# Batch 1's attention moved beside group 0's mixer, with loads reordered, v spread in 32-row tiles, and filler matmuls

## The chip, the cores and the metric

The kernel runs on one core of a Trainium2 chip. The metric is the device time of one execution in microseconds, lower is better. A core has five engines with a queue each: TensorE (PE, with its weight loads shown as PEld), VectorE (DVE), ScalarE (ACT), GpSimd (POOL) and SyncE (SP). Each engine works through its queue in order, and engines wait for each other by semaphores. POOL issues the loads that change float32 to bf16; SP issues the other DMAs.

## The reference

Selective attention for 8 batches, 8 heads, 576 positions and head size 64, followed by a mixer on the heads put together (8 x 576 x 512):

```python
cum = np.cumsum(np.maximum(s, 0.0), axis=-1)
bias = -(cum[:, :, :, None] - cum[:, :, None, :])
scores = np.where(causal, -1e9, q @ k.T / np.sqrt(D) + np.minimum(bias, 0.0))
x = softmax(scores) @ v                    # heads side by side: (B, S, 512)
u = x + ((x.transpose(0, 2, 1) @ U) @ V).transpose(0, 2, 1)   # rank 32 over positions
out = u + np.maximum(u @ w_ch1, 0.0) @ w_ch2                   # 512 -> 2048 -> 512
```

`causal` marks the keys behind a query's position.

## The kernel before

Attention goes by pairs of heads: pair `n` is two heads of batch `n // 4`, 32 pairs in all. A pair has three parts, written as generators that hand back control (`yield`) between pieces:

- `transposes(n)`: 16 PE transposes turn q and k (loaded as 72 partitions x 8 rows) into the pair's slot, one of five; the results go from PSUM to the slot by four copies of 64x576, on ACT or DVE as `copies` says. Four more rows of the slot hold the bias: for batch 0 SP copies them from `rows`, later from `rows_hbm`.
- `scores(n)`: for each head one step of 1024 columns, then one step for both heads (`mid`) and a small one (`tail`). ACT makes exp of each into `pT`; a causal mask follows, on POOL for pairs 1 to 3, on DVE elsewhere. Scores use two PSUM buffers (`pscore`); everything else on PE shares four (`pwork`).
- `values(n)`: 30 matmuls with the head's v, whose extra column of ones gives the sum; DVE divides.

When a batch is through, `seqmix(b)` makes the mix over positions (rank 32) and writes u, transposed, into groups of 512 positions (`uT`). Batch 0 has its own form, `mix_first`, one quarter of the 512 channels at a time. `chanmix(g)` is the channel mixer of a group: 16 hidden steps (4 matmuls of 512 columns each, then a relu on ACT), then four output tiles of 16 matmuls in steps of four. Group 0 adds u by four identity matmuls, later groups by DVE.

`chanmix` runs as filler between the pieces of attention. `run(gen)` calls `step_fill` after each piece, and the pace says how many of 8 calls do a step of the oldest chanmix in `fill`. Before, the pace is 3 of 8 in batch 1, 7 of 8 later, and all at the end. Batch 0 is written out by hand (`step`, `drain`), with `spin_some` for filler matmuls on constant data.

v of batch 0 comes by rows of 4 positions per partition (`v_raw`, and `v_raw_end` for the last 64), and `v_tile(j)` spreads it to 128-position tiles with a selecting matrix `sel`: four matmuls of 512 columns, 128 rows deep (16 for the last). Other batches load v straight into `v_slots` in pieces of one head's row. U, V, w1 in halves, w2 whole, then q and k of batch 1 follow v of batch 0 in POOL's queue; v of batch 1 is issued when batch 0's mix is through, and then q, k and v of batch 2.

The order of PE and POOL is the order in which the program is written, for the whole kernel. DVE, ACT and SP are held to it only up to the call of `in_program_order` behind batch 0; a scheduler orders the rest. POOL's loads use eight semaphores in turn, so a load's issue waits for the landing of the eighth load before it.

Of the kernel before, what the change touches and what calls it, by code (L numbers as in the profile page):

```python
# [39 lines left out]
def kernel(  # L40
# [29 lines left out]
    FT = 2  # L70
# [23 lines left out]
    v_raw_end = v_early[:16, 2048:4096].rearrange("p (h t d) -> p h t d", h=H, t=4)  # L94
# [18 lines left out]
    def ones(ap):  # L113
# [24 lines left out]
    nc.gpsimd.dma_start(  # L138
        out=v_raw.rearrange("p h t d -> p h (t d)"),
        in_=v[0, :, 0:512, :].rearrange("h (p t) d -> p h (t d)", t=4),  # L140
    )
    nc.gpsimd.dma_start(
        out=v_raw_end.rearrange("p h t d -> p h (t d)"),
        in_=v[0, :, 512:576, :].rearrange("h (p t) d -> p h (t d)", t=4),
    )

# [13 lines left out]
    nc.vector.memset(keep, 3.0e38)  # L160
    causal(keep, 1, 128)

# [41 lines left out]
    U_sb = consts.tile([128, 5, 128], BF16)  # L204
    V_sb = consts.tile([128, 4, S], BF16)
# [24 lines left out]
    nc.vector.memset(U_sb, 0.0)  # L230
    nc.vector.memset(V_sb[:, 0, :], 0.0)
# [6 lines left out]
    for half in range(2):  # L238
        nc.gpsimd.dma_start(
            out=w1_sb[:, :, ds(half * 1024, 1024)], in_=w1_in[:, :, ds(half * 1024, 1024)]  # L240
        )
    nc.gpsimd.dma_start(out=w2_sb, in_=moe_w_ch2.rearrange("(kt kp) n -> kp kt n", kp=128))
    alloc_qk(1)
    load_qk(1, 0, H)
# [10 lines left out]
    def copies(n, hh, par):  # L255
        b = n // PB
        on_act = n == 0 or (n == 1 and par == 0) or (b == 1 and par == 1)
        return nc.scalar.copy if on_act else nc.vector.tensor_copy

    def transposes(n):  # L260
        b, hp = divmod(n, PB)
        slot = slots[n % NSLOT]
        if b > 0:
# [3 lines left out]
            )  # L267
        for hh in range(2):
            h = 2 * hp + hh
            tp = pwork().bitcast(BF16)[:, : 2 * 4 * TP].rearrange(  # L270
                "p (c t m) -> p c t m", c=2, t=4
            )
            for c, src in enumerate((q_t[b], k_t[b])):
                for t2 in range(4):
                    nc.tensor.transpose(  # L275
                        tp[:, c, t2, :], src[:, h, ds(t2 * 128, 128)], identity[:TP, :TP]
                    )
# [184 lines left out]
    def v_tile(j, copy):  # L462
        src, rows_in = (v_raw, 128) if j < 4 else (v_raw_end, 16)
        pv = pwork()
        for t in range(4):
            nc.tensor.matmul(
                pv.rearrange("p (h d) -> p h d", h=H),
                lhsT=sel[:rows_in, ds((3 + 128 * j if j < 4 else 3) - t, 128)],
                rhs=src[:, :, t, :],
                start=(t == 0),  # L470
                stop=(t == 3),
            )
        copy(v_slots[0][:, j, :, 0:D], pv.rearrange("p (h d) -> p h d", h=H))
# [66 lines left out]

    def chanmix(g, hT=None, done=0):
# [7 lines left out]
        for nf in range(done, NF):  # L549
# [3 lines left out]
            yield  # L553
        for i in range(4):
            f2 = pwork()
            for nf in range(NF):
                nc.tensor.matmul(  # L557
                    f2,
                    lhsT=hT[:, nf, ds(i * 128, 128)],
                    rhs=w2_sb[:, nf, :],  # L560
                    start=(nf == 0),
                    stop=(g > 0 and nf == NF - 1),
                    skip_group_check=True,
                )
                if nf % 4 == 3 and nf < NF - 1:
                    yield
# [25 lines left out]
    pace = [0, 8]  # L592

    def step_fill():
        pace[0] += 1
        if pace[0] % 8 >= pace[1]:
            return
        while fill:
# [17 lines left out]
    def pT_of(n):  # L616
        return pT_early[n - 2] if 2 <= n < PB else pTs[n % 2]

    first_v = v_slots[0]
    nc.vector.memset(first_v[:, 0:4, :, D : D + 1], 1.0)  # L620
# [139 lines left out]
```

## Time and profile before

| what | before |
|---|---|
| median of 6 runs, us | 396.9 (393.95 to 397.84) |
| the profiled execution, us | 396.95 |
| its span, first to last instruction, us | 395.2 |
| mean granted TensorE clock | 0.991 |
| PE busy, us | 374.4 |
| PE weight loads busy, us | 214.1 |
| DVE busy, us | 222.9 |
| ACT busy, us | 194.5 |
| POOL busy, us | 62.4 |

Busy time is the time in which an engine has an instruction under way. Matmuls overlap in PE's pipeline, so a busy PE needn't be at its peak. Times in the text count from the span's start. A stage table gives busy time between two moments; the timeline gives instructions in order, several alike put together, with the idle time before them and what ended it in brackets.

### The profile page before, as it was taken

To read this page: it belongs to the slowest core of one execution; us is meant where nothing else is said; L and a number is where in the kernel's file an instruction comes from. 1 tells how busy PE (TensorE), PEld (TensorE's weight loads), DVE (VectorE), ACT (ScalarE), POOL (GpSimd) and SP (SyncE) were. 2 spreads that over 40 slices of the span, in tenths; PEclk is the share of its full clock that TensorE was granted. 3 is DMA by queue.
4 is the path that set the end of the run, shared out by engine and by line. 5 is a ranking of instruction groups with operands and counts; after the bars stand their busy time and mean duration, and the time that the engine had idled before them with its cause. 6 is when DMAs were issued, how large, how long until landed. Compare 5 with 4: busy or idle time off the path is not lost.

```text
span 395.2 us, 8325 instructions
## 1 busy us (share of the span) xinstructions
PE 374.4 (95%) x3474; PEld 214.1 (54%) x3532; DVE 222.9 (56%) x480; ACT 194.5 (49%) x290; POOL 62.4 (16%) x89
## 2 busy tenths in 40 slices
PE   8899688989999899999999999999999999999995
PEld 3575255755555455555555555455655554444442
DVE  7882045887677766766676667676678352002011
ACT  5865458526733376427632773367434820630610
POOL 8754243200500050005000500000000000000000
PEclk9999969999999999999999999999999999999999
DMA  7999999984995399229932997141224015301002
GB/s 113 184 224 196 153 115 117 177 57 82 125 119 93 83 137 98 75 78 146 112 55 81 136 127 73 57 96 21 46 71 98 17 35 133 81 27 75 6 27 80
DMA packets 89122, 37.78 MB, mean 96 GB/s; under 512 B 70462, under 2 KB 82910, under 8 KB 89086
## 3 DMA queue, kind: packets, MB, share of 16 engines
q0 software_dynamic: 50416, 18.44, 58.9%
q1 hardware_dynamic: 38670, 18.82, 24.6%
q8 instruction: 27, 0.44, 0.5%
q14 instruction: 9, 0.07, 0.1%
HBM read 37.51 MB, written 9.95 MB: 120 GB/s over the span
## 4 chain that ended last, share of the span: by engine, by line
PE 80%; DMA 10%; DVE 3%; ACT 2%; issue 2%; POOL 2%; DVEq 0%; POOLq 0%
PE pwork L557 31%; PE pwork L533 28%; PE pscore L290 9%; DMA k_sd<-in_k_dram 8%; PE pwork L355 6%; PE pwork L275 3%; DMA hT<-in_v_dram 2%; PE pwork L427 1%; ACT pT L315 1%; DVE o_sb L569 1%; ACT slot L280 1%; POOL q_sd L108 1%; POOL k_sd L108 1%; PE pwork L384 1%; ACT pT L322 0%
## 5 line engine op out<-in xcount | busy, mean ns | idle before, releaser
L552 ACT ACTIVATE hT<-pwork 128x512 bf16<-128x512 f32 x140 | 84.9, 607 | 113.7 <-PE pwork L533 113.7
L557 PE MATMUL pwork<-w_sb,hT 128*128 128x512 bf16 x550 | 138.2, 383 | 2.4 <-ACT slot L280 0.9
L533 PE MATMUL pwork<-uT,w_sb 128*128 128x512 bf16 x532 | 134.5, 379 | 1.6
L280 DVE COPY slot<-pwork 64x576 bf16<-64x576 bf16 x114 | 90.7, 799 | 22.0 <-PE pwork L275 19.0
L315 ACT ACTIVATE pT<-pscore 128x1024 bf16<-128x1024 f32 x60 | 61.1, 1026 | 48.1 <-PE pscore L290 47.9
L557 PEld LDWEIGHTS <-hT 128*128 128x128 bf16 x576 | 51.6, 98 | 52.5 <-issue 3.1
L533 PEld LDWEIGHTS <-w_sb 128*128 128x128 bf16 x576 | 50.4, 98 | 48.3 <-DVE uT L409 0.3
L290 PEld LDWEIGHTS <-slot 68*128 68x128 bf16 x576 | 44.2, 98 | 29.6 <-issue 2.9
L290 PE MATMUL pscore<-slot 68*128 68x128 bf16 (+4 forms) x512 | 57.6, 248 | 1.9 <-DMA slot<-hT 0.9
L302 DVE TENSOR_TENSOR pT<-pT,keep 128x512 bf16<-128x512 bf16 (+1 forms) x87 | 30.3, 354 | 51.2 <-ACT pT L315 30.2
L569 DVE TENSOR_TENSOR o_sb<-pwork,u_sd 128x512 f32<-128x512 f32 x32 | 22.1, 691 | 63.1 <-PE pwork L557 45.5
L355 PEld LDWEIGHTS <-pT 128*128 128x128 bf16 x900 | 33.6, 97 | 10.6 <-DVE uT L409 0.7
L355 PE MATMUL pwork<-v_slot,pT 128*128 128x65 bf16 x900 | 35.8, 193 | 0.9 <-DVE o_sb L569 0.5
L322 ACT ACTIVATE pT<-pscore 128x1024 bf16<-128x1024 f32 x30 | 31.2, 1039 | 3.3 <-PE pscore L290 2.7
L365 DVE TENSOR_TENSOR x_sb<-pwork,rec 128x320 bf16<-128x320 f32 x64 | 31.2, 489 | 1.9
L108 POOL DMA_DIRECT2D q_sd<-in_q_dram x11 | 8.7, 793 | 148.1 <-PE pwork L275 137.1
L218 POOL DMA_DIRECT2D v_slot<-in_v_dram x28 | 25.0, 910 | 5.6 <-DMA v_slot<-in_v_dram 2.9
L409 DVE TENSOR_TENSOR uT<-pwork,xT 128x256 bf16<-128x256 f32 (+6 forms) x54 | 19.6, 416 | 6.7 <-PE pwork L427 6.7
L275 PE MATMUL pwork<-identity,k_sd 72*128 72x72 bf16 x256 | 18.8, 199 | 4.0 <-DMA k_sd<-in_k_dram 4.0
L275 PEld LDWEIGHTS <-q_sd 72*128 72x128 bf16 x256 | 15.7, 99 | 12.4 <-issue 1.1
L275 PE MATMUL pwork<-identity,q_sd 72*128 72x72 bf16 x256 | 19.1, 198 | 0.3 <-DVE x_sb L365 0.3
L364 DVE RECIPROCAL rec<-pwork 128x5 f32<-128x5 f32 x64 | 12.1, 190 | 12.2 <-PE pwork L355 11.3
(93 smaller groups left out, 176.1 us busy)
## 6 DMA issues: line engine op xcount, KB each, us to landing
out_dram<-o_sb SPq DMA_DIRECT2D x36, 256.0 KB
q_sd<-in_q_dram POOLq DMA_DIRECT2D x7, 576.0 KB, 9.1
k_sd<-in_k_dram POOLq DMA_DIRECT2D x7, 576.0 KB, 13.8
v_slot<-in_v_dram POOLq DMA_DIRECT2D x28, 128.0 KB, 15.6
w_sb<-in_moe_w_ch_dram POOLq DMA_DIRECT2D x2, 1024.0 KB, 14.5
w_sb<-in_moe_w_ch_dram POOLq DMA_DIRECT2D x1, 2048.0 KB, 28.2
q_sd<-in_q_dram POOLq DMA_DIRECT2D x4, 144.0 KB, 4.8
k_sd<-in_k_dram POOLq DMA_DIRECT2D x4, 144.0 KB, 5.3
```

The source lines that it names most:

```text
L275: nc.tensor.transpose(tp[:, c, t2, :], src[:, h, ds(t2 * 128, 128)], identity[:TP, :TP])
L280: copies(n, hh, par)(dst[:, :, :, :, par], tp[par * D : par * D + D].rearrange("p c t m -> p c m t"),)
L290: nc.tensor.matmul(dst, lhsT=slot[0:KA, hh, ds(S + j * 128, 128)], rhs=slot[0:KA, hh, lo:hi], start=True, stop=True,)
L302: nc.vector.tensor_tensor(dst, dst, keep[:, :, 0:w].to_broadcast([128, n_tiles, w]), op=ALU.min,)
L315: nc.scalar.activation(pT[:, hh, 0:1024], near, EXP, scale=scale)
L322: nc.scalar.activation(pT[:, :, 1024:1536], mid.rearrange("p (a b) -> p a b", a=2), EXP, scale=scale)
L355: nc.tensor.matmul(po[:, i, :], lhsT=pT[:, hh, ds(place(j, i), 128)], rhs=vt[:, j, h, :], start=(j == 0), stop=(j == i), skip_group_check= ...
L365: nc.vector.tensor_tensor(x_sb[:, hp, :, ds(hh * D, D)], po[:, :, 0:D], rec.to_broadcast([128, 5, D]), op=ALU.mult,)
L533: nc.tensor.matmul(f1, lhsT=w1_sb[:, kt, ds(nf * 128, 128)], rhs=u[:, kt, :], start=(kt == 0), stop=(kt == 3),)
L552: nc.scalar.activation(hT[:, nf, :], f1, RELU)
L557: nc.tensor.matmul(f2, lhsT=hT[:, nf, ds(i * 128, 128)], rhs=w2_sb[:, nf, :], start=(nf == 0), stop=(g > 0 and nf == NF - 1), skip_group_c ...
L569: nc.vector.tensor_tensor(o_sb.rearrange("p (a b) -> p a b", a=4), f2.rearrange("p (a b) -> p a b", a=4), u_sd[:, :, i, :], op=ALU.add,)
```

## The change

- Batch 1: the order is written out. Three hidden steps of group 0 instead of twelve run alone, then transposes, scores, v tiles and values of batch 1 with the rest of `chanmix(0)` at 8 of 16 calls; pair 8's scores alternate with `seqmix(1)`. Its output tiles 0 and 1 are begun with the first half of w2.
- The pace is a sum (`pace[0] += pace[1]`, a step at 16): 13 of 16 from batch 2 on.
- Loads: w1's first half, q and k of heads 0 to 3 of batch 1, w1's second half, w2 in two halves, q and k of heads 4 to 7. v of batch 1 comes as `v_raw`, and is spread by PE as batch 0's is.
- `v_tiles` replaces `v_tile`: tile j uses only its 32 rows of `v_raw`, and tiles go two at a time with their matmuls alternating; the end tile is 32 rows deep with two matmuls. Copies are on DVE or ACT as the call says.
- Batch 0: q's transposes of a pair stand ahead of k's, slot copies are shared by head between ACT and DVE, memsets move from DVE to POOL, the mix's steps are shifted by one, and 45 filler matmuls stand where 25 stood.
- The clearing and filling of V_sb's other rows stand behind `in_program_order`, and behind the load of `v_raw` for batch 1.

```diff
-    nc.vector.memset(keep, 3.0e38)
+    U_sb = consts.tile([128, 5, 128], BF16)
+    V_sb = consts.tile([128, 4, S], BF16)
+    nc.gpsimd.memset(keep, 3.0e38)
     causal(keep, 1, 128)
+    nc.gpsimd.memset(U_sb, 0.0)
+    nc.gpsimd.memset(V_sb[:, 0, :], 0.0)
...
+    load_v_raw(0)
...
-    for half in range(2):
+    def load_w1(half):
...
-    nc.gpsimd.dma_start(out=w2_sb, in_=moe_w_ch2.rearrange("(kt kp) n -> kp kt n", kp=128))
+    def load_w2(half):
...
+    load_w1(0)
     alloc_qk(1)
-    load_qk(1, 0, H)
+    load_qk(1, 0, 4)
+    load_w1(1)
+    load_w2(0)
+    load_w2(1)
+    load_qk(1, 4, 4)
...
-        on_act = n == 0 or (n == 1 and par == 0) or (b == 1 and par == 1)
+        on_act = hh == 0 and (n < 2 or b == 1)
...
+        if b == 0:
+            for hh in range(2):
+                turn(hh, 0)
+            yield
         for hh in range(2):
...
+            if b > 0:
+                turn(hh, 0)
+            turn(hh, 1)
...
-    def v_tile(j, copy):
-        src, rows_in = (v_raw, 128) if j < 4 else (v_raw_end, 16)
-        pv = pwork()
+    def v_tiles(b, js, copies):
+        vt = v_slots[b % 3]
+        pvs = [pwork() for _ in js]
         for t in range(4):
...
+            for j, pv in zip(js, pvs):
+                if j < 4:
+                    pick, src = sel[ds(32 * j, 32), ds(3 + 128 * j - t, 128)], v_raw[ds(32 * j, 32)]
+                elif t < 2:
+                    pick, src = sel[:32, 3 - 2 * t : 3 - 2 * t + 256 : 2], v_raw_end
+                else:
+                    continue
+                nc.tensor.matmul(
+                    pv.rearrange("p (h d) -> p h d", h=H),
+                    lhsT=pick,
+                    rhs=src[:, :, t, :],
...
+        for j, pv, copy in zip(js, pvs, copies):
+            n_rows = 128 if j < 4 else 64
+            copy(vt[:n_rows, j, :, 0:D], pv[:n_rows].rearrange("p (h d) -> p h d", h=H))
...
+        ahead = {}
+        if g == 0:
+            for i in range(2):
+                ahead[i] = pwork()
+                for _ in outputs(ahead[i], hT, i, range(8)):
+                    yield
+                yield
...
     def step_fill():
-        pace[0] += 1
-        if pace[0] % 8 >= pace[1]:
+        pace[0] += pace[1]
+        if pace[0] < 16:
             return
+        pace[0] -= 16
...
     def pT_of(n):
-        return pT_early[n - 2] if 2 <= n < PB else pTs[n % 2]
+        if n < PB + 3:
+            return pTs[n % 2] if n % PB < 2 else pT_early[n % PB - 2]
+        return pTs[(n + 1) % 2]
...
-    for pT in (*pTs, pT_early[0]):
-        nc.vector.memset(pT[:, :, 1600:], 1.0)
+    init_v(nc.gpsimd, first_v)
+    for pT in (*pTs, pT_early[0]):
+        nc.gpsimd.memset(pT[:, :, 1600:], 1.0)
...
     spin_some(9)
-    for n, spins in ((0, (2, 4)), (1, (3, 3))):
-        for hh, _ in enumerate(transposes(n)):
-            spin_some(spins[hh])
-    drain(transposes(2))
-    step(S0, S0)
+    step(T0)
+    spin_some(2)
+    step(T0, T0)
+    spin_some(8)
+    step(T1)
+    spin_some(4)
+    step(T1, T1)
+    spin_some(6)
+    step(S0)
+    spin_some(1, pwork)
+    step(S0, T2)
+    spin_some(1, pwork)
+    step(T2, T2)
     spin_some(1, pwork)
     step(S0, S0)
+    spin_some(2, pwork)
+    step(T3)
     spin_some(1, pwork)
-    step(S1)
-    drain(transposes(3))
+    step(T3, T3, S1)
+    spin_some(2, pwork)
     step(S1)
     spin_some(2, pwork)
     step(S1, S1)
-    v_tile(0, dve)
+    spin_some(2, pwork)
     step(S2)
-    v_tile(1, dve)
+    spin_some(2, pwork)
+    v_tiles(0, (0, 1), (dve, dve))
     step(S2)
-    v_tile(2, dve)
+    spin_some(1, pwork)
+    v_tiles(0, (2, 3), (act, act))
     step(S2, S2)
-    v_tile(3, dve)
...
+    spin_some(1, pwork)
+    v_tiles(0, (4,), (dve,))
+    nc.gpsimd.memset(pT_early[1][:, :, 1600:], 1.0)
+    step(S3, S3)
...
+    step(M2)
     hidden_first(0)
-    step(M2, M3)
+    step(M3)
     hidden_first(1)
...
+    in_program_order(tc, traced, [E.DVE, E.Activation, E.SP])
+    load_v_raw(1)
+    init_v(nc.gpsimd, v_slots[1])
     nc.gpsimd.memset(V_sb[:, 1:4, :], 0.0)
...
-    in_program_order(tc, traced, [E.DVE, E.Activation, E.SP])
-    load_v(1)
...
+    fill_with(3)
     pace[1] = 8
-    fill_with(12)
-    pace[1] = 3
     run(transposes(PB))
-    for n in range(PB, NP + 2):
+    run(transposes(PB + 1))
+    run(scores(PB, pT_of(PB)))
+    run(transposes(PB + 2))
+    run(scores(PB + 1, pT_of(PB + 1)))
+    run(transposes(PB + 3))
+    run(scores(PB + 2, pT_of(PB + 2)))
+    for js in ((0, 1), (2, 3), (4,)):
+        v_tiles(1, js, (act, dve))
+        step_fill()
+    run(values(PB, pT_of(PB)))
+    run(transposes(2 * PB))
+    run(scores(PB + 3, pT_of(PB + 3)))
+    run(values(PB + 1, pT_of(PB + 1)))
+    run(values(PB + 2, pT_of(PB + 2)))
+    run(values(PB + 3, pT_of(PB + 3)))
+    run(transposes(2 * PB + 1))
+    first, mix = scores(2 * PB, pT_of(2 * PB)), seqmix(1)
+    for _ in range(4):
+        step(first)
+        step_fill()
+        step(mix)
+        step_fill()
+    run(mix)
+    fill.append(chanmix(1))
+    pace[1] = 13
+    for n in range(2 * PB, NP + 2):
...
-                pace[1] = 7
-    pace[1] = 8
+    pace[1] = 16
```

## The prediction

> **What bounds the kernel now.** I read the page's slices first, then a table of stages, then the timeline inside the stages that aren't full, because a share over the whole span (95% PE) hides where the time could come from.
>
> ```profile
> span 395.2 us, 8325 instructions
> PE   8899688989999899999999999999999999999995
> PEclk9999969999999999999999999999999999999999
> ```
>
> PE is at nine tenths from slice 10 on. What the change can win lies in the first 90 us, and in what little is loose behind them. The stage table (columns: PE, PEld, DVE, ACT, POOL busy us with counts, granted clock, DMA share, GB/s):
>
> ```profile
> 12.10:27.20 15.10, 14.14 (x177) 9.40 (x179) 13.11 (x25) 12.52 (x16) 8.68 (x14) 1.00 1.19 210
> 35.30:45.50 10.20, 10.15 (x54) 4.66 (x52) 1.33 (x4) 7.80 (x13) 0.83 (x1) 1.00 1.78 183
> 45.50:49.70 4.20, 0.55 (x8) 0.31 (x7) 0.00 (x0) 0.72 (x2) 1.61 (x4) 1.00 3.47 122
> 49.70:58.60 8.90, 7.74 (x61) 4.34 (x63) 3.68 (x6) 4.99 (x6) 3.90 (x5) 0.62 2.56 113
> 58.60:72.40 13.80, 12.45 (x177) 8.55 (x176) 8.34 (x21) 10.67 (x14) 6.21 (x8) 1.00 2.12 130
> 88.70:391.30 302.60, 296.29 (x2628) 166.01 (x2676) 168.66 (x354) 142.25 (x220) 23.54 (x28) 1.00 0.62 80
> ```
>
> At 35.3 batch 0 is done and twelve hidden steps run alone; from 45.5 PE waits for k of batch 1, which lands at 49.6; behind the wait the clock is 0.62. At 88.7 both kernels will have done the same set of work: group 0's mixer, values of pairs 4 to 7, seqmix(1), scores up to pair 8, transposes up to pair 9. So I predict when that point comes, and then what the last 302.6 us lose or gain.
>
> Per matmul in dense stretches: 0.216 us for 512 columns (four of L533 in 0.86 us), 30 of L355 in 0.91, 12 of L290 in 0.89, 8 transposes in 0.26. From 35.3 to 88.7 the work by these prices is: 28 fill steps of 0.86 and four identity groups of 0.22, 25.1; five pairs of scores at 1.38, 6.9; six of transposes at 0.52, 3.1; four of values, 3.6; seqmix(1) 2.8: 41.5 of 53.4 us. So 11.9 us is loose: 4.2 waiting, about 3 the slow clock, the rest like this:
>
> ```profile
> 58.62 1.02 ACT L322 ACTIVATE pT<-pscore 128x1024 bf16<-128x1024 f32 x1 [0.62 <-PE pscore L290]
> 59.54 0.27 ACT L328 ACTIVATE pT<-pwork 128x128 bf16<-128x128 f32 x1
> 59.83 0.80 ACT L280 COPY slot<-pwork 64x576 bf16<-64x576 bf16 x1
> 60.66 1.02 ACT L315 ACTIVATE pT<-pscore 128x1024 bf16<-128x1024 f32 x1
> 61.71 0.80 ACT L280 COPY slot<-pwork 64x576 bf16<-64x576 bf16 x1
> 62.53 1.02 ACT L315 ACTIVATE pT<-pscore 128x1024 bf16<-128x1024 f32 x1
> 63.45 1.02 ACT L322 ACTIVATE pT<-pscore 128x1024 bf16<-128x1024 f32 x1
> ```
>
> ACT stands end to end: a pair of batch 1 costs it 3.35 us of exp and 1.6 of copies, and no hidden step's relu (0.607, L552) is even among them yet. Batch 0's end hangs on ACT too:
>
> ```profile
> 15.88 1.99 ACT L315 ACTIVATE pT<-pscore 128x1024 bf16<-128x1024 f32 x2
> 26.85 0.27 ACT L328 ACTIVATE hT<-pwork 128x128 bf16<-128x128 f32 x1
> 27.18 1.07 PE L355 MATMUL pwork<-v_slot,hT 128*128 128x65 bf16 x30
> 22.96 1.03 PE L466 MATMUL pwork<-hT,sel 16*128 16x512 bf16 x4
> ```
>
> Pair 2's values take the buffer that pair 3's last exp (end 27.12) frees, and start at 27.18. From there to 35.3 PE is full.
>
> **The change part by part.**
>
> *Batch 0.* Pair 0's first exp starts at 12.76 because the first row DMA lands at 12.1; SP still issues those at 8.2, so that stays. Slot copies of pairs 0 and 1 are split between ACT and DVE and end near 11.6, under that wait: no gain. Memsets go from DVE to POOL: nothing, DVE idled there.
> What is new is the PE queue between exps. Pair 2's transposes now stand before pair 0's third score step: it starts 14.45, exp 15.1 instead of 14.65, last exp ends 16.4. Pair 3's transposes stand before pair 1's first scores (they stood behind), and in the built program's waits the second needs the buffer of that last exp (16.4), and the filler between its q and k halves needs the buffer of pair 2's first copies on DVE: those come behind two masks, 15.2 plus two of 0.83, 16.9. So filler 17.1, k half 17.3, scores 17.8, exp 18.0: 2.1 late against 15.88. The 20 added fillers are 4.3 us of PE, mostly under such waits; this one holds the queue, and behind it stand pair 1's scores, for which ACT waits.
> Two v copies go to ACT (0.6 each) into this chain, and v tiles 0 and 1 (then 2 and 3) become one block before the next score. Before, ACT also lost 1.0 to 23.9 waiting for rows_hbm; that is swallowed. Chain with the v blocks at 1.73 each: pair 1 ends 21.3, pair 2's second exp 23.5 to 24.5, v copies to 26.5, pair 2 ends 27.8, pair 3 31.1. Pair 2's values start 31.15, +4.0. M2's second half now follows its first directly and waits 0.4 for DVE's copy. Batch 0 ends 39.7: **+4.4**. POOL, moved past more: w1's second half, w2's two and q/k's second half are issued behind v_raw's landing (about 17.5), five of 0.8, then ten memsets under 2 us: masks from 24; it needs pair 3's last exp only at 31.1, so 7 us of slack. Behind it POOL issues v_raw(1) and clears V_sb (1.54), which DVE copies 0.93 before M3's copy: ready 37.0, M3 asks for it at 36.6: counted in the rounding.
>
> *The v blocks* are the disputed price. Row: L466 above, 16 rows deep, four in 1.03 with 0.38 the last one's own: 0.217 each, no cheaper than with 128 rows. The Trainium skill, TensorE: Matmul & The Clock Gate (Part 3), says tiles on different row groups run concurrently, 3.07 times for four; TensorEngine Tiling (Key Properties) says a change of tiling mode drains TensorE. Ends: 0.86 and 1.73 per pair. At 0.86 pair 3's exps end 30.0 and batch 0 is +3.3, and batch 1's tiles cost 1.7 less. The trace has no two row groups side by side; I take 1.73, the row, and keep 0.86 for the range: 2.8 us in all.
>
> *Batch 1, part A.* Call batch 0's end P. Three hidden steps, then transposes and scores of pairs 4 to 6 with nine more. The 4.2 us wait and the slow clock go: k of heads 0 to 3 is queued ahead of three quarters of the weights, heads 4 to 7 in the place where all of k was, without v's small pieces: before P+10, when pair 6 asks. What is late next is ACT. Its queue from P+3.4 (relus of the hidden steps before): 8 copies 6.4, 9 relus 5.5, three pairs of exp 10.1, gaps 0.3: 22.3, to P+25.7. PE's own work there is 14.8 us, but two score buffers tie it: pair 6's third step waits for an exp at P+22.8. The clock page (Part 1) drops the clock after an idle window of 3.4 us; the row behind a 4.2 us wait shows 0.62, and 58.6 to 72.4 with ACT leading shows 1.00. Gaps here are near 1 us, so I take 1.00.
>
> *Part B* is PE's from P+23.3: 16 output steps 13.8, identities 0.9, v 3.9, values 3.6, transposes 1.0, two pairs of scores 2.8, seqmix(1) 2.8: 28.9, and 1.2 in waits for v's buffers and copies. End P+53.4, or P+51.7 with cheap tiles. Before: 35.3 + 53.4. So the whole stage gives **0.0**: 12 us of looseness went, 6 came back as ACT's queue, 5 as v, the rest as waits.
>
> *Behind it.* Pace 14/16 becomes 13/16. Per batch 39 calls gave 34.1 steps where a chanmix has 32, so seqmix(2) runs bare:
>
> ```profile
> 130.93 0.23 PE L397 MATMUL pwork<-identity,uxT 128*128 128x128 bf16 x1 [0.64 <-DVE uxT L393]
> 131.54 1.04 PE L427 MATMUL pwork<-V_sb,ux 128*128 128x512 bf16 x4 [0.38 <-DVE ux L399]
> ```
>
> Now 31.7: two output steps stand in these gaps, and one in seqmix(5)'s. PE's waits behind 90 us sum to 3.4; I take **-1.8**, ends -0.5 and -2.5. The tail is dense either way.
>
> Sum: 4.4 + 0.0 - 1.8 = +2.6. The profiled run took 396.95 (span 395.2, 1.75 around it), the median of six is 396.9. So 399.5.
>
> **The rivals.**
> *Cheap tiles, no change.* The v pairs overlap: +3.3 - 1.7 - 1.8 = -0.2, 396.7. For: the page. Against: the row, and three blocks that each change mode twice.
> *Faster.* Batch 0's exp chain isn't held: pair 2's copies on DVE finish before pair 3's filler asks, so pair 1's exp starts by 16.3, 0.4 late. With cheap tiles batch 0 then ends 1.7 sooner: +1.6 - 1.7 - 1.8 = -1.9, and fewer waits in part B than my 1.2 make -2.5: 394.5. It decides at 17 us: an exp of pair 1 before that, and it is faster. Against: the two masks and 0.83 a copy are rows of this trace.
> *Slower by more.* 14.8 of 20.7 us busy is too little, and the clock falls in part A: PE's work doubles to 29.6 there, 9 beyond ACT's: up to 405. For: the 0.62 row. Against: 1.00 from 58.6 on.
> *It doesn't do what it says.* k of heads 4 to 7 still comes at 49.6, as k does now; pair 6 asks at 50, so even that costs nothing.
>
> **How the numbers follow.** The sum as it stands, 0.37; cheap tiles, 0.27; the chain unheld, 0.28; the clock, 0.08. A measurement of this kernel can tell about 0.5%, 2 us. Faster by more 0.28, within 0.27, slower 0.45. The sum's own range is 396.7 to 402 (tiles 2.8 down, 2.5 up for stalls in A and B that I set at 1.2 and the fill). The range of 8 in 10 reaches to the unheld chain with a larger gain behind, 393.0, and into the clock's case, 403.5.
>
> **What would show it.** Right: pair 1's first exp near 18, pair 3's last near 30 to 31, batch 0's end near 39, ACT without gaps for 22 us behind it, no wait for k, granted clock 1.00 from 40 on, the common point at 91 to 93, seqmix(2) with no gap over 0.3. Wrong: pair 1's exp before 17, ACT with gaps in part A, eight v matmuls in under 1 us, or a slice of PEclk under 9.

## The result, and the profile after

The changed kernel takes 392.6 us (median of 29 runs, 391.81 to 396.45) against 396.45 (66 runs, 393.76 to 398.4). The medians differ by 3.9 us; the ratio of the means is 0.9916, 95% interval 0.99 to 0.9932: about 3.3 us faster. The ratios, here and below, leave out executions over 1.5% above the fastest of their kernel, which only e8 (four of twelve) and e15 (two of six) have. The prediction had 399.5, with 393.0 as its lower end. The profiled execution took 393.28 us, span 391.6, so the spans differ by 3.6.

The page first: PE's hole in the fifth slice is gone, and with it the lower clock in the sixth.

```profile
span 391.6 us, 8401 instructions
PE   8799879999999999999999999999999999999995
PEclk9999999999999999999999999999999999999999
```

The stage table (columns: PE, PEld, DVE, ACT, POOL busy us with counts, granted clock, DMA share, GB/s) is cut at the changed kernel's own marks: the first scores, the values of pair 2, the end of batch 0, the end of part A, and the common point, which is here the start of pair 10's transposes.

```profile
12.86:29.80 16.94, 15.73 (x202) 10.24 (x204) 11.25 (x21) 13.29 (x18) 12.60 (x25) 1.00 1.21 211
29.80:38.40 8.60, 8.36 (x120) 5.80 (x120) 5.08 (x18) 2.76 (x6) 6.42 (x12) 1.00 1.21 209
38.40:61.40 23.00, 19.51 (x181) 10.93 (x181) 9.69 (x17) 22.57 (x34) 6.79 (x8) 1.00 2.02 169
61.40:88.35 26.95, 25.82 (x320) 16.31 (x324) 20.51 (x47) 8.24 (x11) 3.32 (x4) 1.00 1.52 93
88.35:391.00 302.65, 294.82 (x2638) 165.63 (x2684) 168.81 (x352) 141.75 (x220) 23.50 (x28) 1.00 0.63 81
```

Both kernels have done the same work when pair 10's transposes start. These are the rows of that point, first before and then after, and before's first scores:

```profile
88.24 0.29 PE L275 MATMUL pwork<-identity,q_sd 72*128 72x72 bf16 x4
88.35 0.29 PE L292 MATMUL pwork<-identity,q_sd 72*128 72x72 bf16 x4
12.11 0.62 PE L290 MATMUL pscore<-slot 68*128 68x128 bf16 x6
```

The 88.7 of the prediction is the first hidden step of group 1 (88.74 in that trace), and half of pair 10's transposes stand ahead of it: it is half a us late as a common point. So batch 0 ends at 38.4 (before: 35.3, +3.1). From there to the common point it is 50.0 us (before 52.9, -3.0). Behind it 391.6 - 88.35 = 303.25 us are left (before 395.2 - 88.24 = 306.96, -3.7). The sum is the 3.6 of the spans. Three readings lie behind these three numbers.

Batch 0, from the timeline (start, duration, engine, line, what it does; in brackets the idle time before it and its releaser):

```profile
12.86 0.60 PE L319 MATMUL pscore<-slot 68*128 68x128 bf16 x6 [1.56 <-DMA slot<-hT]
16.80 0.29 PE L292 MATMUL pwork<-identity,q_sd 72*128 72x72 bf16 x4 [0.44 <-ACT pT L357]
17.58 0.38 PE L191 MATMUL pwork<-busy 128*128 128x512 bf16 x1 [0.49 <-DVE slot L309]
18.70 1.94 ACT L344 ACTIVATE pT<-pscore 128x1024 bf16<-128x1024 f32 x2 [1.95 <-PE pscore L319]
21.71 1.08 PE L502 MATMUL pwork<-hT,sel 32*128 32x512 bf16 x8
22.73 0.62 PE L319 MATMUL pscore<-slot 68*128 68x128 bf16 x6
29.86 1.07 PE L384 MATMUL pwork<-v_slot,hT 128*128 128x65 bf16 x30
```

Pair 3's q half waits for the last exp of pair 0, the filler behind it for DVE's copies of pair 2, and pair 1's first exp is late by that: 18.70, with ACT idle for 1.95 us. The eight v matmuls are through in 1.02 us, from 21.71 to the next instruction's 22.73. Pair 2's values start at 29.86. The first row DMA also landed later than before, so the first scores start at 12.86 in place of 12.11; counted from them batch 0 takes 25.5 us in place of 23.2, 2.3 more.

Part A, one period of ACT from the first exp of pair 4 to that of pair 5:

```profile
45.90 1.94 ACT L344 ACTIVATE pT<-pscore 128x1024 bf16<-128x1024 f32 x2
47.71 0.62 ACT L603 ACTIVATE hT<-pwork 128x512 bf16<-128x512 f32 x1
48.19 1.06 ACT L351 ACTIVATE pT<-pscore 128x1024 bf16<-128x1024 f32 x1
49.09 0.32 ACT L357 ACTIVATE pT<-pwork 128x128 bf16<-128x128 f32 x1
49.25 0.65 ACT L603 ACTIVATE hT<-pwork 128x512 bf16<-128x512 f32 x1
49.73 1.65 ACT L309 COPY slot<-pwork 64x576 bf16<-64x576 bf16 x2
51.40 0.60 ACT L603 ACTIVATE hT<-pwork 128x512 bf16<-128x512 f32 x1
51.89 1.93 ACT L344 ACTIVATE pT<-pscore 128x1024 bf16<-128x1024 f32 x2
```

ACT has no gap, as predicted. But the durations of the first seven rows sum to 6.84 us and the period is 5.99: an instruction starts 0.11 to 0.17 before the ACTIVATE ahead of it ends. Behind the two copies there is no such overlap (49.73 + 1.65 = 51.38, next start 51.40).

Behind the common point, all the waits of PE that the table of waits lists (total, times, longest):

```profile
PE pwork L413 <- DVE x_sb L394: 0.4, 1, 0.4
PE pwork L456 <- DVE ux L428: 0.4, 1, 0.4
PE pwork L384 <- DVE uT L438: 0.4, 1, 0.4
PE pwork L479 <- DVE uT L438: 0.3, 1, 0.3
```

That is 1.5 us where 3.4 stood before. At seqmix(2), where before's lines show waits of 0.64 and 0.38, two output steps now stand in the gaps and PE does not wait.

### The profile page after: what moved, and what is told of

Its sections match the earlier page's. It is cut to its first block, busy times and chain, and to the rows that moved or that the text cites. A ratio compares the mean times of both kernels' runs of the same rounds, so it can differ in the third digit from the quotient of the medians.

```text
span 391.6 us, 8401 instructions
## 1 busy us (share of the span) xinstructions
PE 374.2 (96%) x3507; PEld 213.2 (54%) x3568; DVE 224.9 (57%) x472; ACT 193.8 (49%) x293; POOL 64.1 (16%) x99
## 4 chain that ended last, share of the span: by engine, by line
PE 89%; ACT 5%; DVE 2%; issue 1%; DMA 1%; ACTq 0%; DVEq 0%
PE pwork L581 31%; PE pwork L571 29%; PE pscore L319 10%; PE pwork L384 7%; PE pwork L292 3%; PE pwork L456 2%; ACT pT L344 1%; PE pscore L191 1%; PE pwork L502 1%; DMA slot<-hT 1%; ACT hT L603 1%; DVE x_sb L394 1%; PE pscore L571 1%; PE pwork L413 1%; ACT slot L309 1%
## 5 line engine op out<-in xcount | busy, mean ns | idle before, releaser
L571 PE MATMUL pwork<-uT,w_sb 128*128 128x512 bf16 x530 | 136.1, 379 | 2.6 <-ACT pT L357 0.9
L581 PE MATMUL pwork<-w_sb,hT 128*128 128x512 bf16 x548 | 136.0, 379 | 1.4 <-issue 0.2
L309 DVE COPY slot<-pwork 64x576 bf16<-64x576 bf16 x116 | 92.8, 800 | 11.6 <-PE pwork L292 9.8
L344 ACT ACTIVATE pT<-pscore 128x1024 bf16<-128x1024 f32 x58 | 58.6, 1025 | 47.5 <-PE pscore L319 47.1
L319 PE MATMUL pscore<-slot 68*128 68x128 bf16 (+4 forms) x512 | 56.1, 245 | 3.5 <-DMA slot<-hT 1.6
L319 PEld LDWEIGHTS <-slot 68*128 68x128 bf16 x576 | 43.2, 97 | 29.2 <-issue 6.1
L384 PEld LDWEIGHTS <-pT 128*128 128x128 bf16 x870 | 32.8, 98 | 11.3 <-issue 0.8
L384 PE MATMUL pwork<-v_slot,pT 128*128 128x65 bf16 x870 | 35.3, 193 | 0.8 <-DVE uT L438 0.4
L351 ACT ACTIVATE pT<-pscore 128x1024 bf16<-128x1024 f32 x29 | 30.2, 1041 | 2.7 <-PE pscore L319 1.9
L223 POOL DMA_DIRECT2D v_slot<-in_v_dram x24 | 21.3, 902 | 14.1 <-DMA w_sb<-in_moe_w_ch_dram 7.7
L292 PE MATMUL pwork<-identity,q_sd 72*128 72x72 bf16 x256 | 18.3, 197 | 1.0 <-ACT slot L309 0.5
L292 PE MATMUL pwork<-identity,k_sd 72*128 72x72 bf16 x256 | 17.8, 197 | 0.0
```

The lines of the kernel that those rows point to most:

```text
L292: nc.tensor.transpose(tps[hh][:, c, t2, :], src[:, 2 * hp + hh, ds(t2 * 128, 128)], identity[:TP, :TP],)
L309: copies(n, hh, par)(dst[:, :, :, :, par], tp[par * D : par * D + D].rearrange("p c t m -> p c m t"),)
L319: nc.tensor.matmul(dst, lhsT=slot[0:KA, hh, ds(S + j * 128, 128)], rhs=slot[0:KA, hh, lo:hi], start=True, stop=True,)
L344: nc.scalar.activation(pT[:, hh, 0:1024], near, EXP, scale=scale)
L351: nc.scalar.activation(pT[:, :, 1024:1536], mid.rearrange("p (a b) -> p a b", a=2), EXP, scale=scale)
L384: nc.tensor.matmul(po[:, i, :], lhsT=pT[:, hh, ds(place(j, i), 128)], rhs=vt[:, j, h, :], start=(j == 0), stop=(j == i), skip_group_check= ...
```

## The experiments

Ratios are of means, to the kernel before as it ran beside each, with 95% intervals; the changed kernel itself has 0.9916. "P" is the end of batch 0.

| run | median us | ratio |
|---|---|---|
| e1 changed, pace 14/16 | 394.33 | 0.9955 [0.9936, 0.9975] |
| e2 before, pace 13/16 | 392.36 | 0.9893 [0.9851, 0.9936] |
| e3 changed, pair 3's transposes one step later | 392.04 | 0.9888 [0.9857, 0.9919] |
| e4 changed, v blocks tile by tile | 392.42 | 0.9899 [0.9868, 0.9929] |
| e5 changed, old order in batch 0 | 391.47 | 0.9897 [0.9866, 0.9929] |
| e6 changed, without fillers | 396.25 | 1.0001 [0.9979, 1.0023] |
| e7 before, k early | 392.15 | 0.9914 [0.9886, 0.9941] |
| e8 changed, v pair on the same 32 rows | 398.1 | 1.0021 [0.9989, 1.0052] |
| e9 before, k early and pace 13/16 | 387.99 | 0.9799 [0.9762, 0.9836] |
| e10 changed, plain v ahead of V_sb | 398.31 | 1.0049 [1.0027, 1.0071] |
| e11 = e5 with q, k of heads 4-7 ahead of w2 | 390.97 | 0.9868 [0.9834, 0.9902] |
| e12 = e11 with e10's load | 396.46 | 1.0008 [0.9984, 1.0032] |
| e13 changed, plain v behind V_sb | 390.18 | 0.9853 [0.9827, 0.988] |
| e14 changed, batch 1's copies on DVE | 390.11 | 0.9861 [0.9834, 0.9889] |
| e15 = e9 with paired v tiles in batch 0 | 389.84 | 0.9815 [0.9769, 0.9862] |
| e16 = e13, e14 and q, k ahead of w2 | 392.16 | 0.9885 [0.9843, 0.9927] |
| e17 = e16 with the old order in batch 0 | 393.09 | 0.9928 [0.9902, 0.9954] |

### The pace alone, both ways

```diff
 # e1, on the changed kernel
-    pace[1] = 13
+    pace[1] = 14
 # e2, on the kernel before
-                pace[1] = 7
+                pace[:] = [0, 13]
```

In e2 the step is counted in sixteenths from there on; the 3/8 of batch 1 stays.

> The changed kernel with its steady pace of 13/16 put back to 14/16, nothing else. Theory (pace): the 3.25 us gained behind the common point at 88.35 come from the slower pace, which leaves output steps for the waits of seqmix(2) and seqmix(5). Then 1.8 to 3.3 us come back: about 394.4 to 396, ratio to the kernel before 0.995 to 0.999, and seqmix(2) shows PE waits of 0.4 to 0.6 us for DVE's uxT and ux again. Rival (the gain behind is the clock's or comes from another order of the first 88 us): under 0.5 us lost, 392.6 to 393.1, ratio 0.991 to 0.993.

> The kernel before with one part of the change alone: from group 1 on the pace 13/16 in place of 7/8; the 3/8 of batch 1 stays as it was. Theory (pace): it gains what the changed kernel gained behind 88 us, 1.8 to 3.3 us: 393.2 to 394.7, ratio 0.992 to 0.9955; everything before 88.7 stays. Rival: the pace is worth under 0.5 us by itself, ratio 0.999 to 1.0.

e1 loses 1.7 us by the medians and 1.9 behind the common point (393.8 - 88.63 = 305.17, against 303.25). The wait of seqmix(2) is back: here are e1's common point and its step of seqmix(2), and the same step in the changed kernel.

```profile
88.63 0.30 PE L292 MATMUL pwork<-identity,q_sd 72*128 72x72 bf16 x4
130.71 0.23 PE L426 MATMUL pwork<-identity,uxT 128*128 128x128 bf16 x1 [0.56 <-DVE uxT L422]
128.99 0.22 PE L426 MATMUL pwork<-identity,uxT 128*128 128x128 bf16 x1
```

e2's span is 391.3, 3.9 us under before's. This is its common point:

```profile
87.40 0.30 PE L275 MATMUL pwork<-identity,q_sd 72*128 72x72 bf16 x4
```

Behind it 303.90 us follow in place of 306.96: 3.1 us. The other 0.8, ahead of it, is not the edit's, as nothing there was changed; it is how far two executions of the same work differ. The pace is a gain by itself, and by the medians it is worth as much in the kernel before as the whole change. But e2 also sets the counter to 0 there. Counted from the calls, the changed kernel and e1 come to this point with 0 too, the kernel before with 3 of 8. So e1 changes the pace alone, e2 the pace and this phase; the phase alone was not run.

### The order of loads alone, and with the pace

```diff
 # e7, on the kernel before; e9 adds e2's pace
-    for half in range(2): ...w1 half...
-    nc.gpsimd.dma_start(out=w2_sb, ...)
-    alloc_qk(1)
-    load_qk(1, 0, H)
+    load_w1(0)
+    alloc_qk(1)
+    load_qk(1, 0, 4)
+    load_w1(1)
+    nc.gpsimd.dma_start(out=w2_sb, ...)
+    load_qk(1, 4, 4)
```

> The kernel before with the order of loads alone changed: q and k of heads 0 to 3 of batch 1 stand behind the first half of w1, those of heads 4 to 7 behind w2, as in the changed kernel; v of batch 1, the program order of batch 1 and the pace 7/8 stay. Theory (wait and clock): the 4.2 us that PE waits for k at 45.5 go and with them the stretch at clock 0.62 (about 3 us); ACT's queue takes some of it back: the common point comes 3 to 6 us before 88.7, time 391 to 394, ratio 0.984 to 0.993. Rival (the wait is only moved: ACT's end to end work of batch 1 beside a pace of 3/8, or k of heads 4 to 7 at 49.6, holds PE): under 1.5 us, ratio 0.996 to 1.0.

> The kernel before with two parts of the change and no other: the order of loads (k of heads 0 to 3 early) and the pace 13/16 from group 1 on. Batch 0's order, v of batch 1 by plain loads, and batch 1's program order with its pace of 3/8 stay as before. By the profiles the loads took 6.0 us from the first 88 us and nothing behind them, the pace 3.7 behind and nothing ahead. Theory (the parts add, and what else the change does costs what is missing): span 395.2 - 6.0 - 3.7 = 385.5, time about 387.3, up to 390 in runs where a wait slows the clock; ratio 0.976 to 0.984, 4 us or more below the changed kernel. Rival (both parts fill the same looseness, so one eats the other): 390.5 to 392, ratio 0.986 to 0.990.

e7's common point is the first row here, e9's the second:

```profile
82.21 0.30 PE L279 MATMUL pwork<-identity,q_sd 72*128 72x72 bf16 x4
82.79 0.30 PE L279 MATMUL pwork<-identity,q_sd 72*128 72x72 bf16 x4
```

In e7 it comes 6.0 us before 88.24, with nothing behind it changed (389.2 - 82.21 = 307.0). Its runs spread with the clock: 390.8 to 390.9 where the mean granted clock was 1.0, 393.7 to 394.1 where it was 0.99, and all runs of the kernel before lie at 0.982 to 0.995. In e9 the two gains add but for about half a us: span 386.7, 5.5 us sooner at the common point and 303.9 behind it, 3.1 less than before. At 388.0 us e9 beats both kernels: the changed one by 4.6 us. So load order and pace give more than the change has in all, and what else it does costs 4.6.

### What else it does: batch 0's order

```diff
 # e3: one step moved
-    step(T3)
-    spin_some(1, pwork)
-    step(T3, T3, S1)
+    step(S1)
+    step(T3)
+    spin_some(1, pwork)
+    step(T3, T3)
 # e5: the order of the kernel before
-    spin_some(6)
-    step(S0)
...
-    step(T3, T3, S1)
-    spin_some(2, pwork)
-    step(S1)
+    step(T2, T2, T2)
+    spin_some(4)
+    step(S0, S0)
+    spin_some(1, pwork)
+    step(S0, S0)
+    spin_some(1, pwork)
+    step(S1)
+    step(T3, T3, T3)
+    step(S1)
 # e11: e5, and in the loads
+    load_qk(1, 4, 4)
     load_w2(0)
     load_w2(1)
-    load_qk(1, 4, 4)
```

> The changed kernel with pair 3's transposes and the filler between their halves behind the first scores of pair 1, where they stood before; pair 2's transposes and all fillers stay. Theory (held queue): that block holds pair 1's scores on PE for DVE's copies. Without it pair 1's first exp starts at 16.5 to 17.0 in place of 18.70, pair 3's last exp ends 1 to 2 us before 29.80, batch 0 ends 1 to 2 us before 38.39, and as the stage behind it is full, the time falls by the same: 390.6 to 391.6, ratio 0.9865 to 0.989. Rival (the v copies on ACT and the v blocks cost batch 0 its 3.1 us, or the block is only late elsewhere): batch 0's end moves by under 0.5 us, ratio 0.990 to 0.993.

> The changed kernel with the order of the kernel before at the head of batch 0: pair 2's transposes ahead of pair 0's scores, under the wait for the row DMA; pair 3's in one piece behind pair 1's first scores, with no filler between their halves; one filler where there were one or two. The v blocks, and all behind them, stay as changed. Theory (held queue): what delays pair 1 is the filler and the q half of pair 3's transposes, which wait for pair 2's copies. Pair 1's first exp then starts at 15.9 to 16.7 with the second directly behind it, batch 0 ends 1.5 to 2.4 us sooner than the 37.7 to 38.4 of the changed kernel, and the time is 390.3 to 391.2, ratio 0.984 to 0.988. Rival (once pair 1 comes sooner, the v blocks and the two v copies on ACT, or v_raw's landing, hold pair 2): batch 0's end moves by under 0.7 us, time 392 to 392.6.

> The changed kernel with the old order at the head of batch 0 (as in the run with the old turns) and with q and k of heads 4 to 7 of batch 1 queued ahead of w2. In the run with the old turns PE waited 1.92 us for q of heads 4 to 7 at 46.3 to 48.2 and the granted clock behind it was 0.79 and 0.53 in two stretches of 5 us. Theory (the 2 us won in batch 0 ran into that transfer): now the wait is gone, clock 1.00 throughout, and the time is 390 to 390.8, ratio 0.983 to 0.986, in every run. Rival (another wait comes in its place, w2's above all): 391.3 to 393.

e3 was a miss. Its timeline shows ACT:

```profile
16.09 1.03 ACT L344 ACTIVATE pT<-pscore 128x1024 bf16<-128x1024 f32 x1
18.60 1.02 ACT L344 ACTIVATE pT<-pscore 128x1024 bf16<-128x1024 f32 x1 [1.48 <-PE pscore L319]
```

The first exp of pair 1 came sooner, as expected, but the second stood behind the same block, so the hold had only moved: P is 37.59, and 37.67 in e4, where this order isn't touched. Both differ from the changed kernel's 38.39 mostly because the row DMA landed 0.5 to 0.7 us sooner; counted from the first scores batch 0 takes 25.3 us in e3 and 25.5 in the other two. In e5 the copies are early, since pair 2's transposes lie under the wait for that DMA: exps of pair 1 from 15.74 without a gap, P = 36.18, 2.2 us sooner, of which 0.65 is the row DMA's (24.0 us from the first scores, 1.6 less). By the medians 1.1 us of it are left. The timeline, and e5's stages of 5 us:

```profile
48.20 0.42 PE L292 MATMUL pwork<-identity,q_sd 72*128 72x72 bf16 x4 [1.92 <-DMA q_sd<-in_q_dram]
45.00:50.00 5.00, 3.08 (x28) 1.75 (x26) 1.35 (x4) 3.69 (x7) 2.45 (x3) 0.79 1.59 182
50.00:55.00 5.00, 5.00 (x25) 2.68 (x24) 1.91 (x4) 3.54 (x5) 0.87 (x2) 0.53 1.83 179
```

Pair 6's transposes now ask for q of heads 4 to 7 before it lands at 48.2, and the clock falls behind the wait. (In the changed kernel's profile it lands at about 47.0 and is asked for at 48.33.) This profile is of the slowest of e5's six executions, 393.9 us at a mean clock of 0.991; the two at 1.0 took 390.8 and 390.9. With that transfer ahead of w2 (e11) the wait is gone, the clock is 0.996 or more in every run, and 390.97 is 1.6 us under the changed kernel, a little above the 390 to 390.8 expected: PE waits 1.2 us for ux_first there. That is about the 1.6 us that the order takes from batch 0.

### The fillers

```diff
 # e6: between step(S0) and step(S3, S3)
-    spin_some(1, pwork)   (and all others there: 16 matmuls, one less than the expectation counts)
```

> The changed kernel without the 17 filler matmuls between pair 0's first scores and pair 3's (those ahead of pair 0's scores stay). Theory (the fillers hold the queue a little and keep nothing up): pair 1's first exp at 17.3 to 17.7 in place of 18.0 to 18.7, batch 0 ends 0.3 to 1 us sooner, granted clock 1.00 in every slice, time 391.6 to 392.3. Rival (the fillers keep the clock): slices 1 to 4 of the granted clock fall under 9, batch 0 ends 1 us or more later, time 393.5 or more.

The rival held. Pair 1's first exp starts at 16.53, 2.2 us sooner than in the changed kernel, and yet batch 0 ends 2.3 us later (40.73) and 3.7 us are lost. The first row is a stretch of the changed kernel, the second the same stretch of e6, and behind them are e6's stages of 3 us:

```profile
14.00:17.40 3.40, 2.59 (x36) 1.68 (x35) 2.31 (x4) 2.63 (x4) 2.37 (x4) 1.00 1.49 219
14.00:17.40 3.40, 1.72 (x32) 1.34 (x30) 2.92 (x5) 2.32 (x4) 2.46 (x5) 0.97 1.49 231
15.00:18.00 3.00, 1.83 (x27) 1.43 (x27) 2.94 (x4) 1.92 (x4) 2.06 (x3) 0.86 1.45 260
18.00:21.00 3.00, 3.00 (x19) 1.56 (x17) 2.91 (x6) 2.58 (x4) 2.93 (x5) 0.50 1.08 198
21.00:24.00 3.00, 3.00 (x17) 0.98 (x14) 1.78 (x3) 1.02 (x1) 2.94 (x11) 0.50 1.16 212
27.00:30.00 3.00, 3.00 (x41) 2.55 (x39) 0.99 (x3) 1.94 (x2) 1.36 (x4) 0.50 1.15 211
```

The last column but two is the granted clock: 0.50 from 18 to 30. No single wait of PE's ahead of the drop is longer than 1.21 us, but PE was busy for only 1.72 of the 3.4 us from 14.0 to 17.4, against 2.59 in the changed kernel. All twelve runs have a mean clock of 0.974 to 0.982.

### The v blocks

```diff
 # e4: the two loops exchanged
-        for t in range(4):
-            for j, pv in zip(js, pvs):
+        for j, pv in zip(js, pvs):
+            for t in range(4):
 # e8: both tiles of a block from one row group
+                    at = 32 * (j - j % 2)
-                    pick, src = sel[ds(32 * j, 32), ...], v_raw[ds(32 * j, 32)]
+                    pick, src = sel[ds(at, 32), ...], v_raw[ds(at, 32)]
```

> The changed kernel with the two loops of a v block exchanged: the four matmuls of the first tile, then the four of the second, so that neighbours are on the same 32 rows. Same instructions, same count. Theory (two row groups run beside each other): the block of 8, which took 0.98 to 1.02 us from its start to the next instruction's, takes 1.6 to 1.75; two blocks in batch 0, where pair 2's scores stand behind them and ACT waits, and two in batch 1 where PE is the bound: 1.5 to 3 us more, 394 to 395.5, ratio 0.995 to 0.999. Rival (a matmul of 32 rows is cheap by itself, and the order does not matter): the block stays at 1.0, time 392.6, ratio 0.991 to 0.993.

> The changed kernel with both tiles of a v block taken from the same 32 rows, so v's tiles 1 and 3 get other rows of v; count, shapes and order of the instructions stay, only the second tile's row group is the first's. Theory (two row groups run beside each other, whatever the order): on one group the 8 matmuls run one after the other, 0.216 us apart: the block takes 1.73 us in place of 0.98 to 1.02, pair 2's second scores come 0.75 us later, batch 0 ends 0.7 to 1.5 us later and batch 1's blocks cost 1.5 more: time 394 to 395.3. Rival (a 32-row matmul is cheap by itself): the block stays at 1.0, time 392.2 to 392.8.

The timelines of e4 (first two rows) and e8:

```profile
20.99 1.08 PE L502 MATMUL pwork<-hT,sel 32*128 32x512 bf16 x8
22.00 0.61 PE L319 MATMUL pscore<-slot 68*128 68x128 bf16 x6
21.69 1.90 PE L503 MATMUL pwork<-hT,sel 32*128 32x512 bf16 x8
23.52 0.62 PE L319 MATMUL pscore<-slot 68*128 68x128 bf16 x6
```

On one row group the block takes 1.83 us, on two 1.01, whatever the order in the program: e4's 1.6 to 1.75 was a miss, and e8's row is from a stretch with a clock of 1.00 (21 to 24 us). Two row groups do run beside each other, and a 32-row matmul is not cheap by itself. e8's two runs with a mean clock of 0.998 or more took 394.65 and 395.94, in and just above the 394 to 395.3 expected; the others had 0.978 to 0.996.

### v of batch 1, and ACT's copies

```diff
 # e10; e13 puts load_v(1) behind the V_sb copies instead
-    load_v_raw(1)
-    init_v(nc.gpsimd, v_slots[1])
+    load_v(1)
     nc.gpsimd.memset(V_sb[:, 1:4, :], 0.0)
...
-        v_tiles(1, js, (act, dve))
 # e14
-        on_act = hh == 0 and (n < 2 or b == 1)
+        on_act = hh == 0 and n < 2
```

> The changed kernel with batch 1's v by plain loads into its v buffer, as before, in place of v_raw and three blocks of 32-row tiles; fill steps and all else stay. Theory (v's blocks in batch 1 are paid on PE): 18 matmuls, 2.9 us from 60.40 to 63.28, go and nothing takes their place: common point near 85.5, time 389.5 to 390.3, ratio 0.982 to 0.985. Rival (v's small pieces come late and hold values of pair 4, or delay q and k of batch 2): PE waits for v's landing near 63 and the time stays at 392 or rises.

> The three edits together on the changed kernel: old turns in batch 0, q and k of heads 4 to 7 ahead of w2, batch 1's v by plain loads. If the prices add: 2 us from batch 0 and 2.9 from v: 387.3 to 388.5, ratio 0.977 to 0.980. If batch 1 is held by ACT's queue or by loads once PE has less to do: 389.5 to 391.

> The changed kernel with batch 1's v by plain loads as in the kernel before, now issued behind the clearing of V_sb and its copies, and without the three v blocks. Theory (v's blocks cost PE 2.9 us between 60.40 and 63.28): no wait for ux_first, v lands before values of pair 4 at 63, common point near 85.5, 389.5 to 390.3, ratio 0.982 to 0.985. Rival (the plain pieces of v land late[...]): PE waits for v near 61, 392 to 395, and the blocks on PE are the cheaper way in this order.

> The changed kernel with batch 1's slot copies all on DVE (8 of 0.8 us leave ACT in part A). Theory (ACT leads part A): a pair's period falls from 5.98 towards PE's own 4.9, with the waits of PE on exps (0.72 and 0.26 a pair) shrinking: part A ends 2 to 3 us sooner, time 389.5 to 390.8, ratio 0.982 to 0.986. Rival (PE in order, two score buffers and DVE's four copies in a row of 3.3 us set the period): under 0.7 us, or up to 1 us slower, 392 to 393.5.

e10 and e12 tell nothing of v. e10's wait (8.5 us at the same place in e12) and its row in DVE's timeline show why:

```profile
PE pwork L534 <- DVE ux_first L522: 7.8, 2, 7.6
43.00 0.30 DVE L757 COPY V_sb<-V_sb 32x576 bf16<-32x576 bf16 x1 [9.63 <-POOL V_sb L755]
```

POOL's issues of v wait for the weights' transfers (one of them for 5.0 us), the clearing of V_sb stands behind them, DVE's copies behind that, and PE behind DVE. With the load behind the clearing (e13) 0.8 us of that wait is left, and the common point comes 3.1 us sooner, although P was 39.42 there:

```profile
85.23 0.29 PE L292 MATMUL pwork<-identity,q_sd 72*128 72x72 bf16 x4
```

390.18 is 2.4 us under the changed kernel: that is what putting v of batch 1 together on PE costs (18 matmuls, 60.40 to 63.28), net. The stage behind batch 0 is 4.2 us shorter (85.23 - 39.42, against 49.96), and batch 0 is 1.5 us longer from its first scores (27.0 against 25.5), as DVE's copies of V_sb now stand among the copies that batch 0 waits for.

e14 gains 2.5 us. Its own profile cannot show the period: it is the slowest of its six executions, PE waits 1.6 us for q of heads 4 to 7, and behind that the clock is 0.61 (51 to 54 us). e16, which has the same copies, shows it at a clock of 1.00, by the first exps of pairs 4 to 6 and a relu between them:

```profile
46.00 1.94 ACT L344 ACTIVATE pT<-pscore 128x1024 bf16<-128x1024 f32 x2
50.62 0.60 ACT L603 ACTIVATE hT<-pwork 128x512 bf16<-128x512 f32 x1 [0.62 <-PE pwork L571]
51.12 1.93 ACT L344 ACTIVATE pT<-pscore 128x1024 bf16<-128x1024 f32 x2
56.23 1.93 ACT L344 ACTIVATE hT<-pscore 128x1024 bf16<-128x1024 f32 x2
```

With 1.65 us less on ACT a pair takes 5.12 and 5.11 us in place of 5.99, near the 4.9 expected. So ACT led part A by about 0.9 us a pair, and ACT's wait of 0.62 for PE shows what leads next.

### All together

> The changed kernel, batch 0 as changed (with all fillers), with three edits: q and k of heads 4 to 7 of batch 1 ahead of w2, batch 1's v by plain loads behind the clearing of V_sb, and batch 1's slot copies all on DVE. If the terms are separate: 392.6 - 2.4 - 2.5 = 387.7, ratio 0.977 to 0.980, clock 1.00. If they are one looseness (whatever is taken off, the other holds part A and B): 389.5 to 390.5.

> The same with the old order at the head of batch 0 (pair 2's transposes first, pair 3's behind pair 1's first scores, fewer fillers). If batch 0's 1.6 us is a separate term too: 386.1 us, ratio 0.972 to 0.976, below the kernel before with early k and the slower pace (388.0). If the shorter batch 0 only meets a transfer or loses fillers and clock: 387.5 to 390, runs spread by the clock.

> The kernel before with early k and the pace 13/16 (the best so far, 388.0), and batch 0's v tiles 0 to 3 in two blocks of 32-row tiles side by side, with a filler behind each block. Theory (a block takes 0.98 us where two tiles took 1.74): batch 0's end comes 0.5 to 1.5 us sooner, as ACT's waits of 0.2 to 0.5 between pair 2's and pair 3's exps go: 386.7 to 387.6, ratio 0.976 to 0.979. Rival (ACT's exps set that stretch, or the rest of PE's time becomes idle and the clock falls): 388 to 390.

The gains don't show in full. e16's two runs with a clock of 0.998 or more are 389.17 and 389.32, above the 387.7 of separate terms, and its other four have 0.990 to 0.995 and 392.05 to 393.68. In e16 PE waits 1.5 us for k of batch 2 (without that wait it would be 387.7, an estimate; it was not run) and in e17, which comes there sooner, 5.1:

```profile
66.11 0.42 PE L292 MATMUL pwork<-identity,k_sd 72*128 72x72 bf16 x4 [5.06 <-DMA k_sd<-in_k_dram]
```

The next transfer is what is late, and the clock behind it is 0.50 (64 to 72 us of e17). In e15 the paired tiles do what was expected of them: counted from the first scores batch 0 takes 22.8 us, against 23.5 in e9. Three of its runs took 387.4 to 387.5 with a clock of 0.999 or more, but the other three 392.19 to 395.85 with 0.974 to 0.985. e9 has one such run in six (390.32 at 0.991) and the lower median; whether the paired tiles are what costs e15 its clock, six runs of each don't show.

## Why the prediction was wrong

The three terms were +4.4, 0.0 and -1.8; they measured +3.1, -3.0 and -3.7. The sign was lost in the second and third. (The prediction's 88.7 is half a us late as a common point; from 88.24 its own working gives the second +0.5.)

*Batch 0 (+4.4, measured +3.1): the mechanism was right, one price was not.* The filler between pair 3's halves waited for DVE's copies (17.58; foretold 17.1), pair 1's first exp came at 18.70 (foretold 18.0, with the row DMA 0.75 later than before), P at 38.4 (39.7). A v block was taken at 1.73 from a row of one tile after another, and measured at 1.02. The Trainium skill, TensorE: Matmul & The Clock Gate (Part 3), was weighed there and set aside for the nearest row; e8 against e4 shows that it was right. A row of the same instruction was not the nearest row, because what differed, the row group of the neighbour, was the point of the change. By the prediction's own working, which gives 1.1 us for 0.86, the blocks account for about 0.9 (an estimate). The rest of the miss was larger than it looks, and the late row DMA hid it, by luck: from the first scores batch 0 grew by 2.3. That leaves about 1.2 us whose cause is open. What was not costed at all is the fillers' gain: they were priced at what they hold, and e6 shows that without them this order loses 3.7 us.

*The stage behind it (0.0, measured -3.0): the step that failed is the sum of ACT's queue.* It added whole durations: 22.3 us from P + 3.4 to P + 25.7. ACT was end to end as foretold, but through at 61.38, P + 23.0, and a pair took 5.99 us and not 6.75. The prediction's own lines showed it: exps of 1.02 us at 62.53 and 63.45 start 0.92 apart. The Trainium skill, ScalarE: Activation LUTs (What ACT_TABLE_LOAD costs), says that back-to-back ACTIVATEs overlap by about 93 ns; here it is 0.11 to 0.17 us for each. So PE came to part B, its first output step, at 59.43, which is P + 21.0 and not P + 23.3: 2.3 us. Part B then took 28.9 us and not 30.1, where the two cheap v blocks account for up to 1.4 (twice 1.73 less 1.02). Together that is the 3.4 us by which the foretold P + 53.4 was missed. e16 shows from the other side that ACT led part A: with its copies on DVE a pair takes 5.1 us. That the wait for k and its clock would go was right, and e7 prices it at 6.0 us in a kernel that does not spend it elsewhere; what came back was counted too high.

*Behind the common point (-1.8, measured -3.7): the pace was sized right, and a second part was put at nothing.* With the pace alone put back, e1 loses 1.9 of the 3.7 us. The other 1.8 is what e1 gains over the kernel before at the same pace; 0.6 of it is there by seqmix(2) (42.1 us from the common point in e1, 42.7 before). The prediction had nothing for it: "the tail is dense either way". What it is stays open. The phase of the fill counter differs between e1 and the kernel before and was not run alone; but e2 and the changed kernel, with the same pace and phase, are still 0.65 us apart (303.90 and 303.25), so it is not the phase alone. By waits, 1.9 of the 3.7 us are in PE's table, and the rest is not.

*The range.* With cheap tiles and 2.3 us off ACT's queue the working gives 3.3 - 1.7 - 2.3 - 1.8 = -2.5: 394.4. The lower end of 393.0 was built from cheap tiles and an unheld chain; ACT's overlap and the second part behind the common point were in no rival.

*The rivals.* "Cheap tiles" had the price right and the sum wrong. "Faster" had the direction, but not its reason: the chain was held, and pair 1's first exp came at 18.70, not by 16.3. So that it came out faster is luck for that rival. The clock in part A did not fall (1.00 from 38.4 to 61.4). Of "it doesn't do what it says": q of heads 4 to 7 landed at about 47.0 and was asked for at 48.33, so the cover that the prediction named was there in this profile, but it is thin: in e3 and e4 PE waits 0.2 to 0.3 us for it, in e14 1.6. Of the four signs of being wrong only the v blocks came, and barely (1.02 and 0.98 us in batch 0); of the signs of being right, ACT's 22 us without a gap were 19.7, and the common point came at 88.35 in place of 91 to 93.

*What stays open.* The rest of the change costs 4.6 us against e9. Taken one at a time, v on PE is 2.4, batch 0's order 1.6 and ACT's copies 2.5, more than 4.6 together; e16 and e17 show that, taken together, they end on the loads of batch 2, but not in which shares.

## What to carry to other kernels

Ask of each part of a change what it gives alone: here two small ones, an order of loads and a pace, gave 8.5 us by the medians, and the large rearrangement around them took 4.6 of it back. For an engine that runs end to end, take the distance from start to start in the timeline, not the mean duration. And where a faster stage meets a transfer or an idle PE, price the wait twice: once itself, once for the clock behind it.

## What the hardware showed

- Matmuls on two groups of 32 rows run beside each other even when the program has all four of one group ahead of all four of the other: 1.01 us for eight, as when they alternate; 1.83 on one group (e4, e8).
- The granted clock halves without any long wait: in e6 behind 3.4 us in which PE was busy for 1.72, no gap over 1.21 us, and it stays at 0.50 for about 12 us though PE is busy throughout. With 2.59 of the same 3.4 us busy it held (the changed kernel). The Trainium skill, TensorE: Matmul & The Clock Gate (Part 1), speaks of an idle window of about 3.4 us; here a stretch of that length, half busy, was enough.
- The spread of a kernel's runs followed the clock in e7 (3.2 us, 1.0 to 0.99) and e15 (8.5 us, 1.0 to 0.974). In the changed kernel the two executions at 0.985 took 396.3 and 396.5 us, all others, at 0.997 or more, at most 394.3. In the kernel before it did not: executions at 0.986 took 394.5 to 398.5 us.
